# Batch 4's q transposed by DMA from SBUF to SBUF, and a new order of all engines from the first product of h on

## The chip, the cores and the metric

The kernel runs on one core of one Trainium2 chip. The core has a matrix engine (TensorE, PE in the profile; its weight loads are PEld), a vector engine (VectorE, DVE), an engine for activations (ScalarE, ACT), GpSimd (POOL) and SyncE (SP). Here POOL and SP do little but issue DMAs. All DMAs are served by 16 DMA engines. The matrix engine reads from SBUF and writes to PSUM, which has 8 banks of 2 KB per partition; VectorE and ScalarE carry results out of PSUM.

The metric is the device time of one execution in microseconds, as the median of several runs. Beside it stands one profiled execution, from which the durations come.

## The reference

Eight batches, eight heads, 576 positions, head dimension 64; the model width is 8 x 64 = 512 and the inner width 1024.

```python
kv  = einsum('bhsd,bhse->bhde', k, v)           # 64 x 64 for each batch and head
out = einsum('bhsd,bhde->bhse', q, kv)
rms = sqrt(mean(out * out, axis=-1) + 1e-06)
x   = (out / rms * g_norm)                      # then (b, s, 512)
h   = maximum(x @ w_in, 0)                      # (b, 576, 1024)
c   = conv_w[0]*h[s-1] + conv_w[1]*h[s] + conv_w[2]*h[s+1]
y   = (h * sigmoid(c)) @ w_out                  # (b, 576, 512)
```

All inputs and the output are float32; the kernel works in bfloat16 with float32 sums.

## The kernel before, in words

**Layout.** For each batch q, k and v are loaded by GpSimd with a cast to bfloat16 as `[96, heads, 6*64]`: partition p holds positions 6p to 6p+5. k and v are in the form that `kv` wants. q has to be transposed, so that the head dimension lies on partitions. Heads go in pairs: t = 0 to 3 is a pair, u = 0 or 1 is two pairs.

**The stages for one batch b**, each a small function whose name is used in the order:

- `Lq`, `Lk`, `Lv` (line 300): one load of 576 KB each (batch 1 in two halves). `Li` and `Lo` load the weights w_in (four parts) and w_out (two parts).
- `qt`/`qtp` (407): TensorE transposes of one u into PSUM; batches in `QP` use `by_parity` (387), 12 transposes of 96x128. `qc` (416) copies the result to the SBUF tile `qT`, on VectorE or (with `:1`) on ScalarE.
- `dq` (437): in place of `qt` and `qc`, for the batches in `QD`: SyncE issues one DMA transpose of one u from the SBUF tile of q to the SBUF tile `qT`.
- `kv` (352): 48 small matmuls into one bank. `kvn` (444) and `ky` (456) copy the result to SBUF, straight and with the halves exchanged; `kx` does the exchange by DMA instead.
- `oq` (460): the product of q and kv for one pair. `sq` (491) squares it on ScalarE, `oc` (500) copies it to SBUF.
- `ss` (570), `ln` (584), `sl` (590), `sp` (600): the sums of squares, the reciprocal root, its split in two bfloat16 parts, and its spread over partitions by TensorE. `mu` (625) multiplies and writes x. For batches 6 and 7 the factor goes through DRAM (`fw`, `fr`). Batches 0 and 1 use an older path (`ot`, `on`, `nl`, `mu0`).
- `hm` (637): one 128-wide slice f of h for a batch, 8 matmuls. `ha` and `hb` are the same in two parts. `re` (671) is the relu, on ScalarE or (`:1`) VectorE.
- `ta` (697), `aa` (706), `ab` (712): the convolution on VectorE; `sg` (739) the sigmoid on ScalarE; `mg` (751) the product with h. These go in five groups c of one or two batches.
- `om` (759): one output tile of 128 rows, 8 matmuls of 128x512 (for the first and last pair of batches in two halves of 4, `.0` and `.4`); `ea` (768) copies it out of PSUM and `st` (798) stores it from SyncE. The last rows go by `oh`, `eh`, `sh`.
- `unread` (424): matmuls whose result nobody reads (fills).

**What sets the order.** The string `ORDER` (line 68 on) lists every step by name. The loop at line 802 runs through it and issues the instructions; then the program ties each instruction to the one before it on the same engine. So the string is the order of every engine, of SyncE and GpSimd too, whose DMAs go out in that order. A token `name.args:choice@slots` gives the engine choice and the places: banks of PSUM, or slots of a ring of SBUF tiles. A step that takes a slot waits for the last users of that slot. The q tiles of the batches share two slots (`q0`, `q1`), k and v likewise two each, `qT` four, the output rows eight.

Before the change SyncE's list begins with dq.5.0, dq.5.1, a store, dq.7.0. GpSimd's list from batch 2 on is Li.2, Lq.2, Lv.2, Lk.2, Lv.3, Lk.3, Lq.3, Lo.0, Lo.1, Lq.4, Lv.4, Lk.4, Lq.5, Lv.5, Lk.5, Lq.7, Lv.7, Lk.7, Lv.6, Lk.6, Lq.6. Lq.7 takes q's slot 0, which batch 4 held; Lq.6 takes slot 1, which batch 5 held.

Of the kernel before, what the change touches and what calls it, by code (L numbers as in the profile page):

```python
# [52 lines left out]
BF16 = mybir.dt.bfloat16  # L53
# [6 lines left out]
QD = (5, 6, 7)  # L60
QP = (2, 3, 4)
# [11 lines left out]
Lq.1.2 ot.0.3@2 sqh.0.3.0@0 mu0.0.2 qt.1.0@0 sqh.0.3.1 onh.0.3.0@6 qc.1.0@0 onh.0.3.1 nlh.0.3.0@1 nlh.0.3.1 ha.0.2@4
muh.0.3.1 ha.0.3@0 muh.0.3.0 ps dg.6 Lv.1.2 hm.0.6@6 dg.7 hb.0.2 re.0.2:1 hm.0.7@2 hb.0.3 re.0.6 cm.0.6@4 sg.0.6@0
re.0.7:1 kv.1.0.2@6 kvc.1.0.2.0@0 ta.0.2@1 kvc.1.0.2.1 cm.0.7@2 ot.1.0@4 hm.0.0@6 sg.0.7 re.0.3:1 ta.0.3 aa.0.1
re.0.0:1 unread.3.1@0 ta.0.0@2 sq.1.0@0 on.1.0@2 nl.1.0@0 hm.0.1@0 ot.1.1@6 qt.1.1@2 re.0.1 ab.0.1 kv.1.2.2@0 mu0.1.0
sq.1.1@0 kvc.1.2.2.1 on.1.1@4 qc.1.1@0 kvc.1.2.2.0 ot.1.3@2 mg.0.3 Li.2 ta.0.1 ot.1.2@0 nl.1.1@0 mu0.1.1 hm.0.4@4
sq.1.2@0 sq.1.3@1 Lq.2.0@0 re.0.4 pl on.1.2@6 Lv.2.0@0 aa.0.0 on.1.3@4 nl.1.2@0 ab.0.0 mu0.1.2 nl.1.3@1 hm.0.5@6
qtp.2.0@0 mu0.1.3 re.0.5:1 ha.1.2@4 sg.0.1 hb.1.2 qc.2.0@0 ta.0.4@0 hm.1.6@2 sg.0.3 qtp.2.1@0 Lk.2.0@0 ta.0.5 aa.0.2
sg.0.0 hm.1.1@6 ab.0.2 re.1.2 qc.2.1@1 sg.0.2 ha.1.3@4 ta.1.2@3 re.1.1 sg.0.4 sg.0.5 hb.1.3 mg.0.0 re.1.6 hm.1.7@6  # L80
al.h1@1 kv.2.0.4@0 re.1.7 mg.0.1 re.1.3 kvn.2.0.4:1 ky.2.0.4.1 hm.1.0@2 hm.1.5@6 ky.2.0.4.0 re.1.0 ta.1.6@1 re.1.5
oq.2.0@0 oq.2.1@4 sq.2.0@0 sq.2.1@1 hm.1.4@2 mg.0.2 ta.1.7 ta.1.3 ta.1.0@0 oq.2.2@6 Lv.3.0@1 oc.2.0:1@0 aa.1.3 oc.2.1
# [42 lines left out]
def kernel(  # L125
# [725 lines left out]
```

## Time and profile before

| | us |
|---|---|
| median of 3 runs | 176.46 |
| lowest and highest run | 175.97, 176.98 |
| profiled execution: span | 174.7 |
| last matmul ends, start of the last copy | 171.36 |
| busy PE, DVE, ACT in the span | 164.6, 151.8, 144.0 |

The span is that of the profiled execution, first to last recorded instruction or transfer; the run time stands 1.7 us above it. How to read what follows: a group row names the line of the code, the engine, what is written and read, how often, then busy time and mean duration, then the idle time in front of these instructions. The chain of waits is followed back from the last instruction; in order of time each piece has its start, its length and its place. A DMA issue row ends with the microseconds from the issue to the landing. In queue rows q0 is the queue of GpSimd's loads and q1 that of SyncE's transfers; the share is of 16 engines and can pass 100% because packets overlap.

### The profile page before, as it was taken

Reading aid. Unit: us, or ns where it says so; the run is one execution under the profiler, and the core shown is the slowest. Engines: PE = TensorE matmul, PEld = TensorE weight load, DVE = VectorE, ACT = ScalarE, POOL = GpSimd, SP = SyncE. Lnnn points to the kernel's source line nnn. Section 1 sums busy time; section 2 is a strip of 40 time slices with the busy share of each in tenths; the row PEclk is TensorE's granted clock in tenths of the full one; section 3 lists DMA queues with packets and bytes.
Section 4 is the critical chain, followed back from the end, with each engine's and each line's share of the span. In section 5 each row is a group of like instructions: output and inputs, shape, how many; then the busy total and the mean of one; then the engine's idle time right before and its main releaser. Section 6 shows DMA issues by size and latency. Waiting matters only on the chain.

```text
span 174.7 us, 3978 instructions
## 1 busy us (share of the span) xinstructions
PE 164.6 (94%) x1590; PEld 100.1 (57%) x1607; DVE 151.8 (87%) x248; ACT 144.0 (82%) x224; POOL 30.8 (18%) x54
## 2 busy tenths in 40 slices
PE   6988997899799999999999999999999999999992
PEld 2545765685644687744677774545687654444451
DVE  4166799999999999999999999999989999998520
ACT  4578897999999999999999998999988629766132
POOL 7994705313130001810000000000000000000000
PEclk9999999999999999999999999999999999999999
DMA  5999999999999999999999390477694400076285
GB/s 151 182 186 198 200 202 203 205 204 204 208 203 205 203 204 164 162 196 191 190 203 234 72 261 6 149 188 181 173 268 161 152 0 4 23 277 235 90 322 196
DMA packets 37450, 30.81 MB, mean 176 GB/s; under 512 B 8608, under 2 KB 32952, under 8 KB 37432
## 3 DMA queue, kind: packets, MB, share of 16 engines
q0 software_dynamic: 21760, 15.96, 60.7%
q1 hardware_dynamic: 15632, 14.59, 29.6%
q8 instruction: 12, 0.20, 0.4%
q14 instruction: 6, 0.05, 0.1%
q10 hardware_dynamic: 40, 0.01, 0.0%
HBM read 34.88 MB, written 9.73 MB: 255 GB/s over the span
## 4 chain that ended last, share of the span: by engine, by line
PE 76%; DVE 9%; DMA 4%; POOL 4%; ACT 2%; issue 2%; POOLq 0%; ACTq 0%
PE bank L764 35%; PE bank L643 30%; DMA w_in_sb<-in_moe_w_in_dram 4%; PE bank L361 3%; PE bank L467 2%; DVE taps L703 1%; DVE qT L346 1%; POOL q_sb L245 1%; DVE taps L709 1%; DVE h L754 1%; PE bank L606 1%; DVE taps L702 1%; POOL v_sb L245 1%; POOL k_sb L245 1%; PE bank L781 1%
## 5 line engine op out<-in xcount | busy, mean ns | idle before, releaser
L643 PE MATMUL bank<-xT,w_in_sb 128*128 128x288 bf16 x480 | 63.6, 286 | 0.3 <-ACT root L545 0.2
L764 PE MATMUL bank<-w_out_sb,h 128*128 128x512 bf16 x267 | 62.4, 379 | 0.8 <-issue 0.3
L643 PEld LDWEIGHTS <-w_in_sb 128*128 128x128 bf16 x480 | 46.0, 98 | 14.9 <-issue 1.6
L748 ACT ACTIVATE taps<-taps,cwn 128x1152 bf16<-128x1152 bf16 (+1 forms) x38 | 39.7, 1078 | 7.4 <-DVE taps L715 7.3
L764 PEld LDWEIGHTS <-h 128*128 128x128 bf16 x280 | 26.4, 98 | 31.0 <-issue 1.2
L649 ACT ACTIVATE h<-bank 128x576 bf16<-128x576 f32 x48 | 30.2, 656 | 3.0 <-PE bank L643 2.8
L344 ACT ACTIVATE row<-bank 128x512 f32<-128x512 f32 (+1 forms) x29 | 16.3, 595 | 8.8 <-PE bank L764 6.0
L754 DVE TENSOR_TENSOR h<-h,taps 128x2304 bf16<-128x2304 bf16 (+1 forms) x20 | 22.0, 1109 | 0.6 <-ACT taps L748 0.6
L709 DVE TENSOR_TENSOR taps<-taps 128x2304 bf16<-128x2304 bf16 (+1 forms) x19 | 21.5, 1134 | 0.2
L715 DVE TENSOR_TENSOR taps<-taps,h 128x2304 bf16<-128x2304 bf16 (+1 forms) x19 | 21.5, 1131 | 0.2
L496 ACT ACTIVATE sq<-bank 128x576 bf16<-128x576 f32 x28 | 17.8, 663 | 0.6 <-PE bank L467 0.3
L703 DVE TENSOR_SCALAR taps<-h,cwn 128x1152 bf16<-128x1152 bf16 (+1 forms) x38 | 17.8, 467 | 0.0
L702 DVE TENSOR_SCALAR taps<-h,cwn 128x1152 bf16<-128x1152 bf16 (+1 forms) x38 | 17.4, 457 | 0.3 <-ACT h L649 0.2
L217 ACT ACT_TABLE_LOAD x12 | 15.4, 1283 | 2.6 <-issue 2.4
L651 DVE TENSOR_SCALAR h<-bank 128x576 bf16<-128x576 f32 x16 | 11.8, 752 | 1.7 <-PE bank L643 0.8
L344 ACT ACTIVATE o<-bank 128x576 f32<-128x576 f32 x19 | 12.8, 674 | 0.0
L632 DVE SCALAR_TENSOR_TENSOR xT<-o,cw,bank 128x576 bf16<-128x576 f32 x16 | 12.2, 808 | 0.1
L304 POOL DMA_DIRECT2D q_sb<-in_q_dram x8 | 6.2, 770 | 30.2 <-PE bank L391 29.4
L430 PE MATMUL bank<-fill 128*128 128x512 bf16 x25 | 9.0, 481 | 1.5 <-DVE fill L232 1.5
L346 DVE COPY row<-bank 128x512 f32<-128x512 f32 (+1 forms) x8 | 5.4, 672 | 4.4 <-PE bank L781 2.4
L361 PE MATMUL bank<-v_sb,k_sb 96*64 96x64 bf16 x384 | 8.3, 197 | 0.7 <-ACT sq L496 0.5
L361 PEld LDWEIGHTS <-k_sb 96*64 96x64 bf16 x384 | 7.1, 112 | 2.9 <-issue 2.2
(94 smaller groups left out, 148.8 us busy)
## 6 DMA issues: line engine op xcount, KB each, us to landing
out_dram<-row SPq DMA_DIRECT2D x35, 256.0 KB, 2.6
q_sb<-in_q_dram POOLq DMA_DIRECT2D x6, 576.0 KB, 15.2
v_sb<-in_v_dram POOLq DMA_DIRECT2D x6, 576.0 KB, 14.6
k_sb<-in_k_dram POOLq DMA_DIRECT2D x6, 576.0 KB, 16.6
factor<-factor SPq DMA_DIRECT2D x8, 288.0 KB, 5.4
w_in_sb<-in_moe_w_in_dram POOLq DMA_DIRECT2D x4, 256.0 KB, 9.0
w_out_sb<-in_moe_w_out_dram POOLq DMA_DIRECT2D x2, 512.0 KB, 18.3
q_sb<-in_q_dram POOLq DMA_DIRECT2D x4, 144.0 KB, 4.7
```

What stands on the lines that cost most here:

```text
L344: nc.scalar.activation(to, fr, AX.Copy)
L361: nc.tensor.matmul(ps[i][i * D:(i + 1) * D, t - t0, :], k_sb[:, 2 * t + i, r * D:(r + 1) * D], v_sb[:, 2 * t + i, r * D:(r + 1) * D], star ...
L496: nc.scalar.activation(in_order(b, s), product(b, t), AX.Square)
L643: nc.tensor.matmul(ps[:, e, :HS], w_in_sb[:, t, f * P:(f + 1) * P], x[:, t, e * HS:(e + 1) * HS], start=(t == 0), stop=(t == NT - 1))
L649: nc.scalar.activation(to, fr, AX.Relu)
L702: nc.vector.tensor_scalar_mul(tap[:, 0, f % 2, :n, 8:8 + S], h[:, f], cwn[:, 0, f:f + 1])
L703: nc.vector.tensor_scalar_mul(tap[:, 1, f % 2, :n, :S], h[:, f], cwn[:, 2, f:f + 1])
L709: nc.vector.tensor_add(tap[:, 1, :, :n, :S], tap[:, 0, :, :n, 7:7 + S], tap[:, 1, :, :n, 1:1 + S])
L715: nc.vector.tensor_add(y, y, h[:, 2 * j:2 * j + 2])
L748: nc.scalar.activation(y, y, AX.Sigmoid, scale=cwn[:, 1, f:f + 1])
L754: nc.vector.tensor_mul(h, h, T["tap", c, j][:, 1, :, :n, :S])
L764: nc.tensor.matmul(T["om", p, m], h[:, f, m * P:(m + 1) * P], w_out_sb[:, f, :], start=(f == 0), stop=(f == NF - 1))
```

## The change

Batch 4 moves from the batches whose q TensorE transposes (`QP`) to those whose q is transposed by DMA (`QD`): qtp.4.0, qtp.4.1, qc.4.0 and qc.4.1 go, dq.4.0 and dq.4.1 come. The tiles for kvn and kvx are made ahead of the order for all batches, which issues no instruction. From the first product of h on, the order string is a new one for all engines.

```diff
-QD = (5, 6, 7)
-QP = (2, 3, 4)
+QD = (4, 5, 6, 7)
+QP = (2, 3)
 QUAD = QD + QP
...
+    for b in QUAD:
+        T["kvn", b] = consts.tile([P, NT, D], BF16, name=f"kvn{b}")
+        T["kvx", b] = consts.tile([P, NT, D], BF16, name=f"kvx{b}")
+
     @op
     def kvn(b, t0, n):
-        if t0 == 0:
-            T["kvn", b] = consts.tile([P, NT, D], BF16, name=f"kvn{b}")
-            T["kvx", b] = consts.tile([P, NT, D], BF16, name=f"kvx{b}")
```

The order string is replaced as a whole from ha.0 on. The new lists of the queues, and TensorE's from batch 4's kv to batch 7's:

```
SyncE:  dq.4.0 dq.4.1 dq.5.1 dq.5.0 dq.7.1 st.0.1 dq.7.0 dq.6.0 dq.6.1 st.0.3 st.0.6 st.0.8 st.0.0 kx.7.0.4.0 st.0.7 kx.7.0.4.1 ...
GpSimd: Li.2 Lv.2@0 Lq.2@0 Lk.2@0 Lv.3@1 Lk.3@1 Lq.3@1 Lo.0 Lo.1 Lq.4@0 Lv.4@0 Lk.4@0 Lq.5@1 Lk.5@1 Lv.5@0
        Lq.7@0 Lq.6@1 Lv.7@1 Lk.7@1 Lk.6@0 Lv.6@0
TensorE: kv.4 sp.3.0 hm.2.7 hm.3.5 oq.4.1 oq.4.0 hm.3.4 hm.2.6 hm.3.6 hm.3.3 hm.3.1 oq.4.3 oq.4.2
        kv.5 hm.3.2 om.0.8.0 hm.2.3 oq.5.2 oq.5.0 om.0.6.0 hm.3.7 om.0.8.4 om.0.4.0 oq.5.3 oq.5.1 om.0.6.4
        om.0.5.0 ss.4 ss.5 hm.2.1 om.0.4.4 hm.2.0 om.0.5.4 sp.4.1 kv.7 om.0.7.0 sp.4.0 om.0.7.4 ...
```

dq.4.0 takes qT's slot 0 and dq.4.1 slot 2, after batch 3's products; dq.5.1 takes slot 1, dq.5.0 slot 3. The engine choices differ too: of 64 relus VectorE does 14 (before 16), of 35 row copies 4 (before 7), of 12 copies for batch 0 and 1's kv 7 (before 4), of 8 exchanged copies 4 (before 3). The fill before the last matmuls stands behind them now. At the end of the string:

```diff
-om.3.1.4 eh.3.8.0:1@4 st.2.5 ea.3.2@1 st.3.5 st.3.2 ea.3.3@2 st.3.3 om.3.7.4 ea.3.1@0 unread.1.2@0 sh.3.8.0 ea.3.7@0
-st.3.1 st.3.7 oh.3.8.1 eh.3.8.1 sh.3.8.1
+ea.3.1@3 st.3.1 st.3.6 om.3.7.4 ea.3.7@2 st.3.7 om.3.2.4 ea.3.2@1 st.3.2 oh.3.8.0@2 eh.3.8.0@5 sh.3.8.0 oh.3.8.1
+eh.3.8.1 unread.1.2@7 sh.3.8.1
```

More of the change, by code (lines that the diff above doesn't have):

```diff
@@ L73 @@
[L73 to L82, printed above, removed]
@@ new lines @@
+re.1.2 aa.0.2 ab.0.2 hm.1.5@2 sg.0.1 mg.0.0 hm.1.7@4 re.1.7 Lo.0 qtp.2.1@6 qc.2.1:1@2 hm.1.6@0 re.1.6:1 ta.1.6@2
+ta.1.7 sg.0.4 re.1.5 Lo.1 qtp.2.0@4 qc.2.0@0 kv.2.0.4@6 ky.2.0.4.1 kvn.2.0.4 ky.2.0.4.0 ta.1.2@0 hm.1.1@0 ha.1.3@2
+aa.1.3 sg.0.5 re.1.1 oq.2.2@6 sq.2.2@0 oc.2.2@0 hb.1.3 re.1.3:1 ta.1.3 aa.1.1 hm.1.4@4 re.1.4 ta.1.4@1 ta.1.5 ab.1.3
+oq.2.0@2 sq.2.0@3 oc.2.0@2 ab.1.1 Lq.4.0@0 hm.1.0@6 re.1.0 oq.2.3@4 sq.2.3@2 oc.2.3 unread.3.1@0 kv.3.0.4@2
+ky.3.0.4.1:1 ky.3.0.4.0:1 kvn.3.0.4 aa.1.2 oq.2.1@6 sq.2.1@4 oc.2.1 qtp.3.1@4 qc.3.1@0 qtp.3.0@2 qc.3.0@2 ss.2@6
```

87 lines of the change are left out of this document (46 added, 41 removed).

## The prediction

> **What bounds the kernel now.** First the page: busy times, the slices, the shares of the chain.
>
> ```profile
> PE 164.6 (94%) x1590; PEld 100.1 (57%) x1607; DVE 151.8 (87%) x248; ACT 144.0 (82%) x224; POOL 30.8 (18%) x54
> ...
> GB/s 151 182 186 198 200 202 203 205 204 204 208 203 205 203 204 164 162 196 191 190 203 234 72 261 6 149 188 181 173 268 161 152 0 4 23 277 235 90 322 196
> ...
> PE 76%; DVE 9%; DMA 4%; POOL 4%; ACT 2%; issue 2%; POOLq 0%; ACTq 0%
> ```
>
> TensorE holds the chain for 76% of the span, but DMA stands at 200 to 208 GB/s in slices 5 to 15 (one slice is 4.37 us: 17 to 66 us) without a dip: a saturated resource beside PE. Next the stages, from the busy times by stretch:
>
> ```profile
> 16.50:48.10 31.60, 28.32 (x409) 20.90 (x411) 29.54 (x60) 29.54 (x53) 11.46 (x23) 1.00 1.32 204
> 48.10:80.00 31.90, 31.59 (x340) 18.98 (x343) 31.33 (x53) 31.46 (x54) 6.29 (x8) 1.00 1.27 191
> 171.40:174.70 3.30, 0.00 (x0) 0.92 0.48 173
> ```
>
> Columns: length; PE, PEld, DVE, ACT, POOL busy; granted clock; DMA share; GB/s (the last row is of PE alone). PE idles 31.60 - 28.32 = 3.28 us in the first stage and 0.3 us in the second. So a new order can win at most some 3.3 us there; after 48.1 us only less PE work helps. Then the chain of waits in order of time:
>
> ```profile
> 47.29 0.75 DVE qT L346
> ...
> 59.72 0.88 PE bank L361 x48
> ...
> 68.28 0.51 PE bank L391 x12
> ...
> 80.20 0.60 PE bank L578 x16
> ...
> 85.80 0.88 PE bank L361 x48
> 86.68 0.23 PE bank L606 x4
> ...
> 98.51 0.37 PE bank L467 x8
> ...
> 124.15 13.81 PE bank L643 x112
> ...
> 147.52 10.74 PE bank L764 x49
> ...
> 170.66 0.22 PE bank L430
> ...
> 171.36 0.28 ACT row L344
> ```
>
> Until 48 us the chain is DVE, then PE to the end at 171.36. The L361 rows are kv of batch 4 (59.72) and batch 7 (85.80). Unit prices: a product of h (8 matmuls) 13.81/112 x 8 = 0.99 us; half an output tile (4) 10.74/49 x 4 = 0.88; kv 0.88; one fill 0.22.
>
> Behind the kv's stand the loads. GpSimd's timeline, the DMA issues with their us to landing, SyncE's timeline:
>
> ```profile
> 36.03 0.79 POOL L304 DMA_DIRECT2D q_sb<-in_q_dram  x1 [4.11 <-PE bank L391]
> ...
> 40.69 0.77 POOL L304 DMA_DIRECT2D k_sb<-in_k_dram  x1
> 47.18 0.77 POOL L304 DMA_DIRECT2D q_sb<-in_q_dram  x1 [5.72 <-PE bank L391]
> ...
> 48.80 0.78 POOL L304 DMA_DIRECT2D k_sb<-in_k_dram  x1
> 69.11 0.77 POOL L304 DMA_DIRECT2D q_sb<-in_q_dram  x1 [19.53 <-PE bank L391]
> ...
> 70.63 0.77 POOL L304 DMA_DIRECT2D k_sb<-in_k_dram  x1
> ```
>
> ```profile
> q_sb<-in_q_dram POOLq DMA_DIRECT2D x1, 576.0 KB, 17.3
> ...
> k_sb<-in_k_dram POOLq DMA_DIRECT2D x1, 576.0 KB, 18.4
> ...
> q_sb<-in_q_dram POOLq DMA_DIRECT2D x1, 576.0 KB, 14.7
> ...
> k_sb<-in_k_dram POOLq DMA_DIRECT2D x1, 576.0 KB, 20.2
> ...
> q_sb<-in_q_dram POOLq DMA_DIRECT2D x1, 576.0 KB, 8.0
> ...
> k_sb<-in_k_dram POOLq DMA_DIRECT2D x1, 576.0 KB, 13.5
> ...
> qT<-q_sb SPq DMA_TRANSPOSE x1, 7.9
> ...
> qT<-q_sb SPq DMA_TRANSPOSE x1, 11.6
> ```
>
> ```profile
> 61.94 6.91 SPq L439 DMA_TRANSPOSE qT<-q_sb  x2
> ...
> 77.15 2.20 SPq L439 DMA_TRANSPOSE qT<-q_sb  x1
> ```
>
> Issue plus landing, row by row: q4 53.3, k4 59.1, q5 61.9, k5 69.0, q7 77.1, k7 84.1 us. k4 lands 0.6 us before kv of batch 4, k7 1.7 us before kv of batch 7. The transposes of q5 go out when q5 is there (61.94; first of two: 7.9 us), that of q7 at 77.15; this one has v7, k7 and more loads behind it and takes 11.6.
>
> How loads and transposes share, by queue, in 50 to 60 (loads alone), 84 to 86 (both), 100 to 102 us (transposes alone):
>
> ```profile
> q0 software_dynamic: 2678, 2.02, 130.8%
> ...
> q0 software_dynamic: 377, 0.28, 90.2%
> q1 hardware_dynamic: 378, 0.10, 36.6%
> ...
> q1 hardware_dynamic: 1464, 0.37, 103.8%
> ```
>
> Columns: packets, MB, share. A load of 576 KB (0.59 MB) at 0.202 MB/us is 2.9 us. Beside a transpose loads get 0.14 MB/us, the transpose 0.05: its 0.29 MB then last 5.9 us and cost the loads (0.202 - 0.14) x 5.9 = 0.37 MB, that is **1.8 us each**. Alone a transpose needs 0.29/0.185 = 1.6 us.
>
> **The change part by part.** The sum is against the profiled execution: last matmul 171.36, span 174.72; the median, 176.46, is 1.74 above that span, and I carry the difference over.
>
> *Transposes off TensorE.*
>
> ```profile
> L391 PE MATMUL bank<-ident,q_sb 96*128 96x96 bf16 x72 | 3.9, 206 | 0.1
> ...
> L344 ACT ACTIVATE qT<-bank 128x1152 bf16<-128x1152 bf16 x1 | 1.1, 1130 | 0.0
> ```
>
> Twelve take 0.51 us (68.28), two such groups go: PE -1.02, of the 72 remain 48. ScalarE loses one copy (1.1), VectorE the other; the new order also moves three ea and two re from VectorE to ScalarE, three kvc and a ky back. Both run beside PE; I count nothing. The fill before the last matmuls (170.66) moves behind them: -0.22. PE work in all: -1.24. The kvn tiles made earlier issue nothing.
>
> *The front.* Batch 1's norms and relus are rearranged; batch 2's loads go out earlier. Bounds: nothing to -3.28, the idle. Earlier issue brings nothing, since that queue is full up to k5. I take 0.6: that is by how much kv of batch 4 can come forward before k4's landing at 59.1 ends it, whatever the front wins.
>
> *Two more DMA transposes, and where they stand.* SyncE now has dq.4.0, dq.4.1, dq.5.1, dq.5.0, dq.7.1, one store, dq.7.0, dq.6.0, dq.6.1. dq.4.0 waits for q4 and goes out at 53.3. Before, no transpose was in flight until 61.9. Now v4, k4, q5, k5, v5 stand beside the batch 4 pair, and the batch 5 pair follows when q5 lands.
>
> *Three new waits on GpSimd.* (1) Lv.5 now takes v's slot 0 and waits for kv of batch 4; it goes out near 61 and joins the queue behind k5, so it costs nothing yet. (2) Lq.7 waits for both transposes of q4, no longer for TensorE. (3) **Lq.6 is put ahead of Lv.7, Lk.7, Lk.6 and Lv.6**, and q's slot 1 is free only when dq.5.1 and dq.5.0 have landed. Behind it waits Lk.7, for that kv of batch 7, and behind kv all of PE, in order.
>
> The sum, step by step:
> 1. v5: five loads after 53.3 are 14.5 us, the batch 4 pair 3.6: 71.4. Kv of batch 5 starts at 71.5 (before: 71.0).
> 2. dq.5.0 lands, X: 53.3 + 14.5 + 4 x 1.8 = 75.0. Low end, four at 1.6: 74.2. High end: dq.4.0 11.6 us as the loaded row (64.9), dq.4.1 another 5.9 (70.8), then 4.2 us beside q7 (0.21 MB) and the remaining 0.37 MB alone (2.0): 77.0. I take 75.0; the loads run out near 71, as they did under the 7.9 us row.
> 3. k7: before, from Lq.7's issue at 69.11 to k7's landing at 84.1 were 15.0 us: three loads from an empty queue with one transpose among them. Now the same three follow Lq.6's issue: X + 15.0 = 90.0. Ends: 13.2 without that transpose, 16.8 with another (dq.7.1 and dq.7.0 both fall here).
> 4. PE, without that wait: kv of batch 5 at 71.5, then kv 0.88, five products 4.93, eight half tiles 7.0, four oq (two pairs at 0.37), two sums 0.60, a spread 0.23: 14.4, so kv of batch 7 at 85.9. It waits 4.1 us, to 90.0.
> 5. Rest: before, 171.36 - 85.80 = 85.56. Now one half tile more stands behind kv of batch 7 (om.0.7.0, +0.88) and the fill is gone (-0.22): 86.2. Last matmul 176.2, +4.8.
>
> **176.46 + 4.8 = 181.3 us.** Ends: 74.2 + 13.2 gives 178.7, 77.0 + 16.8 gives 185.1. VectorE and ScalarE gain slack during the wait. dq.4.0 (61 to 65) is wanted by oq near 64, dq.4.1 by 70: a wait of up to 1 us there lies ahead of v5's and is not added. At the end the two last stores go out together; 0 to +0.3, I take 0.
>
> [...]
>
> **The rivals.**
> *Cheap transposes.* Each costs the loads what 0.29 MB of load costs, 1.45 us. X = 53.3 + 14.5 + 5.8 = 73.6, the leg 14.65, k7 88.2, last matmul 174.4: **179.5**. For: alone, 0.185 MB/us is near the loads' 0.202. Against: the row of 84 to 86 us. [...]
>
> *The load of q6 is no wall.* If X + leg stays under 85.9 (dq.5.0 by 71), only v5 counts: 71.5 + 14.4 + 86.2 = 172.1, **177.2**. Against: X would need transposes that cost half.
>
> *Faster: DMA has room.* The transposes slip between the loads at under 0.9 us for all four, v5 is there by 68.7 and dq.5.0 by 68. Then PE sets the end: -1.24 - 0.6, **174.6**. For: PE holds 76% of the chain. Against: the 200 to 208 GB/s. It decides at kv of batch 7: once k7 lands more than 1.8 us behind PE's arrival there, the gain is spent.
>
> *The clock falls in the wait.* The granted clock was 0.92 in the 3.3 us after the last matmul: if it halves, it did so 2.8 us in. A wait of 4.1 us reaches that. With as long a recovery, 2.8 us at half rate, 1.4 are lost: **182.7**. Against: 1.00 in both stage rows; but PE idled there in 3.3 us of short pieces only. [...]
>
> **How the numbers follow.** Forecast 0.46, cheap transposes 0.13, clock 0.12, no wall 0.12, faster 0.17. Faster by over 0.5% is the one case: 0.17. No wall (+0.4%) is mostly within 0.5%, about what a measurement here can tell from no change: 0.10 same, its rest slower: 0.73. The range leaves out the faster case and the top tail: from 176.0, below no wall, to 185.1.
>
> **What would show it.** In the profile after: k_sb's load of batch 7 lands near 90 and TensorE's longest wait, some 4 us, stands before an L361 group, released by DMA k_sb; GpSimd's wait before Lq.6 is for a transpose, near 75 us; L391 has x48; the batch 4 transposes land 8 to 12 us and later after issue. Wrong if the L361 groups start without waits, or if a second wait (a store behind dq.6.1 that keeps an output row's slot) is longer than these.

## The result and the profile after

The change makes the kernel **slower by 10.7%**: 198.6 us median of 4 runs (195.5 to 201.9) against 176.5, ratio 1.107 (95% interval 1.102 to 1.112). In two of these four runs, in some runs of five kernels below with the new front (the profiled ones of e5_front and e17_newfront_early among them) and in one of the kernel before, the mean granted clock was lower (here 0.947, against 0.956 and 0.974) and the time some per cent longer; ratios leave such runs out, and where too few are left the lowest runs are given. The prediction was 181.3 us with a range up to 185.1: the direction was right, the size was not.

The profiled execution of the changed kernel took 195.54 us with a span of 193.7. First its page: busy times, the granted clock by slice, the shares of the chain.

```profile
PE 169.2 (87%) x1566; PEld 100.5 (52%) x1583; DVE 150.6 (78%) x244; ACT 146.9 (76%) x226; POOL 30.2 (16%) x54
...
PEclk9999999999999999999669699999999999999999
...
PE 36%; DMA 28%; DVE 16%; issue 8%; ACT 5%; POOL 4%; SPq 2%; ACTq 0%; POOLq 0%; DVEq 0%
```

TensorE fell from 76% of the chain to 36%, and DMA rose from 4% to 28%. The clock, at nine tenths or more in every slice before, dips in three slices from 92 to 111 us (4.84 us each). TensorE's timeline, with start, length and, in brackets, the wait ahead and its releaser, says where the time went:

```profile
63.34 0.95 PE L361 MATMUL bank<-v_sb,k_sb 96*64 96x64 bf16 x48
...
75.70 0.95 PE L361 MATMUL bank<-v_sb,k_sb 96*64 96x64 bf16 x48 [1.21 <-DMA v_sb<-in_v_dram]
...
93.54 0.39 PE L607 MATMUL bank<-wparts,spread 32*128 32x288 bf16 x1 [3.32 <-ACT row L344]
94.63 0.43 PE L607 MATMUL bank<-wparts,spread 32*128 32x288 bf16 x3 [0.69 <-ACT h L650]
94.98 1.49 PE L361 MATMUL bank<-v_sb,k_sb 96*64 96x64 bf16 x48
...
107.14 0.43 PE L607 MATMUL bank<-wparts,spread 32*128 32x288 bf16 x4 [3.73 <-ACT h L650]
107.68 4.50 PE L644 MATMUL bank<-xT,w_in_sb 128*128 128x288 bf16 x24
...
112.34 0.95 PE L361 MATMUL bank<-v_sb,k_sb 96*64 96x64 bf16 x48
...
188.55 1.91 PE L782 MATMUL bank<-w_out_sb,h 128*128 128x384 bf16 x16
```

The same view of the kernel before, for its four kv groups:

```profile
59.65 0.95 PE L361 MATMUL bank<-v_sb,k_sb 96*64 96x64 bf16 x48
...
70.94 0.95 PE L361 MATMUL bank<-v_sb,k_sb 96*64 96x64 bf16 x48
...
85.73 0.95 PE L361 MATMUL bank<-v_sb,k_sb 96*64 96x64 bf16 x48
...
94.27 0.95 PE L361 MATMUL bank<-v_sb,k_sb 96*64 96x64 bf16 x48
```

So kv of batch 4 starts 3.7 us later than before (63.34 - 59.65), kv of batch 5 4.8 later, kv of batch 7 9.3 later (94.98 - 85.73) and kv of batch 6 18.1 later; the last matmul whose result is used ends at 190.5 and not at 171.4, 19.1 later. Two stretches make 13.3 us of it: 4.5 between batches 5 and 7 and 8.8 between batches 7 and 6. Neither wait there is for a load. The first, 3.32 us, is for a ScalarE row copy (`ea`), the second, 3.73, for a relu behind another row copy. ScalarE's timeline shows what those copies wait for:

```profile
92.89 0.60 ACT L344 ACTIVATE row<-bank 128x512 f32<-128x512 f32 x1 [4.39 <-DMA out_dram<-row]
...
105.95 0.60 ACT L344 ACTIVATE row<-bank 128x512 f32<-128x512 f32 x1 [6.90 <-DMA out_dram<-row]
```

Each copy wants an output row's slot that a store still reads: ea.0.4 waits for st.0.1, ea.0.7 for st.0.8. Why the stores are late is in SyncE's timeline:

```profile
53.32 8.46 SPq L439 DMA_TRANSPOSE qT<-q_sb  x2
64.53 4.53 SPq L439 DMA_TRANSPOSE qT<-q_sb  x2
79.25 3.38 SPq L439 DMA_TRANSPOSE qT<-q_sb  x1
82.73 0.54 SPq L801 DMA_DIRECT2D out_dram<-row  x1
83.39 6.18 SPq L439 DMA_TRANSPOSE qT<-q_sb  x1
89.74 5.82 SPq L439 DMA_TRANSPOSE qT<-q_sb  x1
95.65 4.89 SPq L439 DMA_TRANSPOSE qT<-q_sb  x1
100.59 3.39 SPq L801 DMA_DIRECT2D out_dram<-row  x4
104.08 0.61 SPq L453 DMA_DIRECT2D kvx<-kvn  x1
```

st.0.1 stands behind dq.7.1, which waits for q of batch 7 and goes out at 79.25; the store follows at 82.73. st.0.8 and the crossed kv (kvx) stand behind three more transposes, and these hold SyncE for 6.18 + 5.82 + 4.89 = 16.9 us while the loads of batches 7 and 6 run beside them. How long the transfers then take to land, first for the one store of 82.73, then for the transposes issued from 79 to 101, then for k of batch 7:

```profile
out_dram<-row SPq DMA_DIRECT2D x1, 256.0 KB, 10.1
...
qT<-q_sb SPq DMA_TRANSPOSE x4, 10.9
...
k_sb<-in_k_dram POOLq DMA_DIRECT2D x1, 576.0 KB, 14.1
```

The kernel before, issues from 90 to 104 us, where its last three transposes go out after the loads, two of these stores ahead of them and three behind:

```profile
out_dram<-row SPq DMA_DIRECT2D x5, 256.0 KB, 3.0
...
qT<-q_sb SPq DMA_TRANSPOSE x3, 3.8
```

A store that takes 3 us took 10.1 in the queue behind a transpose and beside the loads: 82.73 + 10.1 = 92.8, just when ScalarE starts again. The place in the queue alone does not do it: the three stores of the kernel before that go out from 101.03 us, right behind two transposes but after the loads, landed in 2.9 us.

The stages after, in the form of the prediction's second fence:

```profile
42.00:52.00 10.00, 6.70 (x122) 4.46 (x122) 9.87 (x22) 8.07 (x15) 1.53 (x2) 1.00 1.28 205
...
90.00:108.00 18.00, 9.93 (x95) 5.58 (x95) 6.75 (x8) 8.17 (x12) 0.00 (x0) 0.79 1.15 213
```

From 90 to 108 TensorE worked 9.93 of 18 us, at a mean granted clock of 0.79. The waits shown above (3.32, 0.69, 3.73) fill the idle 8 but for 0.3 us; the clock is a second loss on top of them.

### The profile page after: what moved, and what is told of

Its sections match the earlier page's. It is cut to its first block, busy times and chain, and to the rows that moved or that the text cites. A ratio compares the mean times of both kernels' runs of the same rounds, so it can differ in the third digit from the quotient of the medians.

```text
span 193.7 us, 3939 instructions
## 1 busy us (share of the span) xinstructions
PE 169.2 (87%) x1566; PEld 100.5 (52%) x1583; DVE 150.6 (78%) x244; ACT 146.9 (76%) x226; POOL 30.2 (16%) x54
## 4 chain that ended last, share of the span: by engine, by line
PE 36%; DMA 28%; DVE 16%; issue 8%; ACT 5%; POOL 4%; SPq 2%; ACTq 0%; POOLq 0%; DVEq 0%
PE bank L765 18%; DMA v_sb<-in_v_dram 14%; PE bank L644 12%; DMA out_dram<-row 7%; DMA w_in_sb<-in_moe_w_in_dram 4%; DMA factor<-factor 3%; DVE taps L703 3%; DVE xT L629 2%; DVE taps L704 2%; DVE taps L716 2%; DVE taps L710 2%; PE bank L361 2%; SPq L801 1%; DVE h L755 1%; POOL q_sb L245 1%
## 5 line engine op out<-in xcount | busy, mean ns | idle before, releaser
L644 PE MATMUL bank<-xT,w_in_sb 128*128 128x288 bf16 x480 | 65.6, 290 | 1.5 <-DVE xT L629 0.6
L765 PE MATMUL bank<-w_out_sb,h 128*128 128x512 bf16 x268 | 64.0, 386 | 1.7 <-ACT rs L588 0.9
L644 PEld LDWEIGHTS <-w_in_sb 128*128 128x128 bf16 x480 | 46.8, 99 | 18.2 <-issue 3.6
L650 ACT ACTIVATE h<-bank 128x576 bf16<-128x576 f32 x50 | 31.5, 656 | 5.0 <-PE bank L644 4.8
L344 ACT ACTIVATE row<-bank 128x512 f32<-128x512 f32 (+2 forms) x33 | 18.5, 586 | 22.0 <-DMA out_dram<-row 11.5
L703 DVE TENSOR_SCALAR taps<-h,cwn 128x1152 bf16<-128x1152 bf16 (+1 forms) x38 | 18.1, 475 | 0.2
L652 DVE TENSOR_SCALAR h<-bank 128x576 bf16<-128x576 f32 x14 | 10.5, 753 | 1.0 <-PE bank L644 0.5
L361 PE MATMUL bank<-v_sb,k_sb 96*64 96x64 bf16 x384 | 8.9, 203 | 2.0 <-DMA v_sb<-in_v_dram 1.4
L361 PEld LDWEIGHTS <-k_sb 96*64 96x64 bf16 x384 | 7.7, 118 | 4.4 <-issue 4.2
L304 POOL DMA_DIRECT2D q_sb<-in_q_dram x8 | 6.0, 750 | 25.7 <-PE bank L391 15.2
L607 PE MATMUL bank<-wparts,spread 32*128 32x288 bf16 x32 | 3.2, 336 | 7.7 <-ACT h L650 4.4
L430 PE MATMUL bank<-fill 128*128 128x512 bf16 x24 | 8.3, 460 | 1.7 <-DVE fill L232 1.5
```

What stands on the lines that cost most here:

```text
L344: nc.scalar.activation(to, fr, AX.Copy)
L361: nc.tensor.matmul(ps[i][i * D:(i + 1) * D, t - t0, :], k_sb[:, 2 * t + i, r * D:(r + 1) * D], v_sb[:, 2 * t + i, r * D:(r + 1) * D], star ...
L644: nc.tensor.matmul(ps[:, e, :HS], w_in_sb[:, t, f * P:(f + 1) * P], x[:, t, e * HS:(e + 1) * HS], start=(t == 0), stop=(t == NT - 1))
L650: nc.scalar.activation(to, fr, AX.Relu)
L703: nc.vector.tensor_scalar_mul(tap[:, 0, f % 2, :n, 8:8 + S], h[:, f], cwn[:, 0, f:f + 1])
L765: nc.tensor.matmul(T["om", p, m], h[:, f, m * P:(m + 1) * P], w_out_sb[:, f, :], start=(f == 0), stop=(f == NF - 1))
```

## Experiments

Each kernel ran beside the kernel before on the same chip. All orders below are edits of the order string. The table gathers where TensorE starts the four kv groups in the profiled execution, and the time.

| kernel | kv 4 | kv 5 | kv 7 | kv 6 | us, median | ratio to before (95%) |
|---|---|---|---|---|---|---|
| before | 59.7 | 70.9 | 85.7 | 94.3 | 176.5 | |
| after | 63.3 | 75.7 | 95.0 | 112.3 | 198.6 | 1.107 (1.102 to 1.112) |
| e1_rows | 65.0 | 76.1 | 93.6 | 104.7 | 193.2 | 1.096 (1.085 to 1.107) |
| e2_loads | 64.7 | 76.0 | 94.3 | 112.3 | 195.3 | 1.108 (1.095 to 1.121) |
| e3_both | 67.1 | 78.2 | 92.9 | 102.4 | 191.1 | 1.084 (1.073 to 1.095) |
| e4_before_dq4 | 59.8 | 72.8 | 89.3 | 97.8 | 180.2 | 1.022 (1.011 to 1.034) |
| e5_front | 69.5 | 80.7 | 95.5 | 104.1 | 184.3 (182.4, 186.1) | |
| e6_rest | 60.2 | 75.0 | 95.1 | 114.3 | 198.8 | 1.123 (1.088 to 1.159) |
| e7_q4pe | 64.8 | 77.2 | 92.9 | 111.7 | 197.7 (195.2, 200.3) | |
| e8_kvx | 64.8 | 75.9 | 90.6 | 101.5 | 190.4 (188.1, 192.6) | |
| e9_syncorder | 63.8 | 75.4 | 92.9 | 104.0 | 186.7 | 1.055 (1.038 to 1.072) |
| e10_sync_loads | 63.5 | 75.5 | 90.2 | 101.0 | 186.4 | 1.053 (1.037 to 1.070) |
| e11_rest_repaired | 60.9 | 75.5 | 91.8 | 101.6 | 185.8 | 1.050 (1.044 to 1.056) |
| e12_before_sync | 59.2 | 70.5 | 89.5 | 100.9 | 182.8 | 1.033 (1.027 to 1.039) |
| e13_v5 | 59.8 | 73.1 | 89.4 | 102.9 | 187.1 | 1.046 (1.027 to 1.066) |
| e14_v5_q4pe | 62.3 | 74.6 | 89.3 | 98.8 | 182.7 | 1.022 (1.004 to 1.040) |
| e15_newfront_q4pe | 65.7 | 78.0 | 92.7 | 102.2 | 189.3 (186.6, 192.1) | |
| e16_q4pe_early | 60.6 | 73.0 | 87.7 | 98.8 | 182.6 | 1.031 (1.025 to 1.037) |
| e17_newfront_early | 66.6 | 80.6 | 95.2 | 104.7 | 188.8 (185.2 to 193.6) | |

### The waits one at a time: rows, loads, both

The theory from the trace: the two stores are the wall. The rival: the load of q of batch 6 ahead of v and k of batch 7, as predicted.

e1_rows gives the two row copies slots of their own, so that no copy waits for those stores:

```diff
-ea.0.4@6
+ea.0.4@8
-ea.0.7@4
+ea.0.7@9
```

> The changed kernel with two more slots for output rows, so that the copies of output tiles 4 and 7 (ea.0.4, ea.0.7) no longer wait for the stores of tiles 1 and 8; every DMA keeps its place. Theory S (stores behind transposes on SyncE hold output rows, ScalarE waits for them 4.4 and 6.9 us, and the clock falls meanwhile): both waits go, PE reaches batch 7's kv near 91 and then waits for k7, which lands near 92.5; after it nothing stops, the clock stays up: 184 to 186. Rival L (the wall of loads that the prediction named): k7 and v6 still set the times, so only a part of the first wait goes: 191 to 194.

Measured 193.2 us, in the range of rival L: the row waits are gone, but little is won. TensorE's waits in e1_rows show their successors (total, times, longest):

```profile
PE bank L361 <- DMA k_sb<-in_k_dram: 2.7, 1, 2.7
PE bank L468 <- DMA kvx<-kvn: 2.5, 1, 2.5
```

The first is for k of batch 7, as rival L has it. The second, at 108.3 us right behind kv of batch 6, is for the crossed kv of batch 7, whose second half goes out on SyncE at 106.07, behind the same transposes and stores. The row slots were only one of the things that the late queue held up.

e2_loads moves one load on GpSimd:

```diff
-Lq.7 Lq.6 Lv.7 Lk.7 Lk.6 Lv.6
+Lq.7 Lv.7 Lk.7 Lq.6 Lk.6 Lv.6
```

> The changed kernel with GpSimd's loads in the order Lq.7, Lv.7, Lk.7, Lq.6, Lk.6, Lv.6 (Lq.6 no longer ahead of batch 7's v and k); SyncE's order kept. Theory S: k7 lands some 6 us earlier, but kv of batch 7 stands behind the wait for the first store, so it gains nothing; q6 lands about 6 us later, with it the two transposes of q6 and the stores behind them, so the wait for tile 8's store grows: 197 to 202. Rival L: kv of batch 7 comes about 4 us earlier and so does the end: 190 to 192.

Measured 195.3 us, no change that these runs could show, and outside both ranges: ScalarE's waits for rows remain and kv of batch 6 starts at 112.3 as before. The load that the prediction made the wall is worth nothing while SyncE is late.

e3_both has both edits.

> Both edits: two more row slots and batch 7's k and v ahead of Lq.6. Theory S with the load wall as a second, smaller wait: kv of batch 7 at 90 to 91 (TensorE's own pace from batch 5's kv at 75.7), and no wait for a store: 181 to 183. Rival L: as e2, 186 to 190, if the stores had only waited where PE waited anyway.

Measured 191.1 us, above both ranges: kv of batch 7 comes at 92.9 without a wait, and the crossed kv takes over:

```profile
PE bank L468 <- DMA kvx<-kvn: 3.3, 1, 3.3
```

e8_kvx adds to e3_both copies from the bank in place of the four kvx transfers:

```diff
-kvn.7.0.4 kx.7.0.4.0 ... kx.7.0.4.1
+kvn.7.0.4 ky.7.0.4.0:1 ky.7.0.4.1
-kvn.6.0.4:1 kx.6.0.4.0 kx.6.0.4.1
+kvn.6.0.4:1 ky.6.0.4.0:1 ky.6.0.4.1
```

> The kernel with both repairs (two more output rows, q of batch 6 behind k of batch 7), and the crossed kv of batches 7 and 6 copied from the bank by ScalarE and VectorE, as in batches 2 to 5, in place of four transfers that stood behind transposes and stores on SyncE. With both repairs alone 191.1 us, with 3.3 us of TensorE's wait put down to these transfers. Theory K (that wait is on the path): 187 to 188.5 us. Rival (the wait gives way to the next one, the transposes that the products of q of batches 7 and 6 want): 190 to 191.5 us.

Measured 188.1 and 192.6 us. The lower run lies in the range of theory K: the wait was on the path, some 2.5 us against the lower run of e3_both (190.7, on another chip).

### SyncE's order alone, and its converse

e9_syncorder moves only SyncE's instructions:

```diff
-dq.4.0 dq.4.1 dq.5.1 dq.5.0 dq.7.1 st.0.1 dq.7.0 dq.6.0 dq.6.1 st.0.3 st.0.6 st.0.8 st.0.0 kx.7.0.4.0 st.0.7 kx.7.0.4.1 kx.6.0.4.0 kx.6.0.4.1
+dq.4.0 dq.4.1 dq.5.1 dq.5.0 st.0.1 dq.7.0 st.0.3 st.0.6 st.0.8 st.0.0 kx.7.0.4.0 st.0.7 kx.7.0.4.1 dq.7.1 kx.6.0.4.0 kx.6.0.4.1 dq.6.0 dq.6.1
```

> The kernel after the change with SyncE's queue alone in another order: the first store goes ahead of the batch 7 transposes, and the second transpose of batch 7 and both of batch 6 go behind the five stores and behind the crossed kv of batch 7 and batch 6, as they stand in the kernel before. Every other engine keeps the order after the change, q of batch 6 is still loaded ahead of v and k of batch 7. Theory S (from 79 us on SyncE's row sets the end: a store and the kvx transfers wait behind transposes that each hold SyncE 5 to 6 us): ScalarE's waits for output rows and TensorE's for kvx go, kv of batch 7 stays at 92 to 93 us, where k of batch 7 lands, kv of batch 6 comes to 101 to 103, and the time to 184 to 187 us. Rival N (another wait stands as late, as after each single repair so far): 190 us or more.

Measured 186.7 us (185.5 and 187.9), in the range of theory S. SyncE's timeline, TensorE's, and a stage of e9_syncorder:

```profile
69.17 0.53 SPq L801 DMA_DIRECT2D out_dram<-row  x1
79.44 2.35 SPq L439 DMA_TRANSPOSE qT<-q_sb  x1
```

```profile
92.90 0.95 PE L361 MATMUL bank<-v_sb,k_sb 96*64 96x64 bf16 x48 [2.78 <-DMA k_sb<-in_k_dram]
```

```profile
90.00:108.00 18.00, 15.22 (x200) 9.62 (x197) 12.92 (x18) 13.13 (x18) 0.00 (x0) 0.91 0.78 160
```

The first store goes out at 69 and not at 83, no wait for a row is left, and kv of batch 6 comes at 104.0 in place of 112.3. TensorE works 15.2 of the 18 us that held 9.9. What remains is the prediction's own wait, 2.78 us for k of batch 7.

e10_sync_loads adds the edit of e2_loads.

> The same order of SyncE, and q of batch 6 loaded behind k of batch 7. If theory S holds and the load of q of batch 6 is the next wall: kv of batch 7 at 89 to 90, 181 to 184 us. If TensorE itself is by then as late as the load (its front is 4 to 5 us behind): no gain over the kernel with SyncE's order alone, 185 to 187 us.

Measured 186.4 us (185.3 and 187.6). In the trace kv of batch 7 starts at 90.2 without a wait, 2.7 us earlier, and the span of the profiled execution is 2.7 us shorter (183.5 against 186.2), but the medians differ by 0.3 only; each kernel had two runs, 2.3 or 2.4 us apart, so a gain up to some 2 us is neither shown nor excluded.

e12_before_sync is the converse, the kernel before with the two queues in the new manner:

```diff
-SyncE:  dq.5.0 dq.5.1 st.0.0 dq.7.0 kx.7.0.4.1 kx.7.0.4.0 st.0.5 st.0.1 dq.7.1 kx.6.0.4.0 kx.6.0.4.1 dq.6.0 dq.6.1
+SyncE:  dq.5.0 dq.5.1 dq.7.0 st.0.0 dq.7.1 dq.6.0 dq.6.1 kx.7.0.4.1 kx.7.0.4.0 st.0.5 st.0.1 kx.6.0.4.0 kx.6.0.4.1
-GpSimd: Lq.7 Lv.7 Lk.7 Lv.6 Lk.6 Lq.6
+GpSimd: Lq.7 Lq.6 Lv.7 Lk.7 Lv.6 Lk.6
```

> The converse: the kernel before the change, batch 4 on TensorE, with only the queues of SyncE and GpSimd in the new manner: q of batch 6 loaded right behind q of batch 7 and ahead of v and k of batch 7, all four transposes of batches 7 and 6 ahead of the crossed kv of batches 7 and 6 and of four of the stores. Theory S: this alone makes the old kernel slower by 6 to 14 us, 182 to 190 us, with TensorE waiting for kvx or for rows behind the transposes. Rival (the order of queues needs the late front or batch 4's transposes to do harm): below 179 us.

Measured 182.8 us, 3.3% over the kernel before (2.7 to 3.9): in the range of theory S. Its ScalarE, TensorE and SyncE timelines repeat the pattern in a kernel with the old front and batch 4 on TensorE:

```profile
88.86 0.60 ACT L344 ACTIVATE row<-bank 128x512 f32<-128x512 f32 x1 [5.01 <-DMA out_dram<-row]
```

```profile
89.51 1.49 PE L361 MATMUL bank<-v_sb,k_sb 96*64 96x64 bf16 x48 [4.16 <-ACT row L344]
```

```profile
78.43 0.59 SPq L800 DMA_DIRECT2D out_dram<-row  x1
79.13 6.76 SPq L439 DMA_TRANSPOSE qT<-q_sb  x1
86.07 5.34 SPq L439 DMA_TRANSPOSE qT<-q_sb  x1
91.50 4.96 SPq L439 DMA_TRANSPOSE qT<-q_sb  x1
```

The store is again about 10 us behind its issue (78.43 to 88.86), and kv of batch 7, which takes 0.95 us elsewhere, takes 1.49 behind the wait of 4.16. The three transposes hold SyncE 17.1 us, as in the changed kernel. The load of q of batch 6 was moved in the same step, but it could account for 1.4 us of this wait at most: TensorE stood from 85.4 to 89.5, and k of batch 7 had landed at 86.8 (73.2 + 13.6). So the order of the two queues does harm in the old kernel too, 5.8 us here, and SyncE's part alone 9 to 10 in the changed kernel (195.5 against 185.5 by the lowest runs).

### Batch 4's transposes by DMA

e4_before_dq4 is the kernel before with batch 4 alone by DMA:

```diff
-QD = (5, 6, 7)
-QP = (2, 3, 4)
+QD = (4, 5, 6, 7)
+QP = (2, 3)
-qtp.4.0@6 qc.4.0:1@0 ... dq.5.0@2 ... dq.5.1@1 ... qtp.4.1@4 qc.4.1@0
+dq.4.0@0 dq.4.1@3 ... dq.5.0@2 ... dq.5.1@1
```

> The kernel before, with nothing but batch 4's q by DMA: dq.4.0 and dq.4.1 first in SyncE's list, qtp.4 and qc.4 gone, the rest of the order as before. If the DMA transposes themselves cost little (theory S: it is the order around them): PE loses 1.0 us of work, batch 5's k lands 2 to 4 us later (71 to 73) and batch 5's kv waits 0 to 2 us: 175.5 to 178. If the transposes beside the loads are the cause: 181 to 186, with oq of batch 4 and kv of batch 5 and 7 all waiting for DMA.

Measured 180.2 us, 2.2% over before (1.1 to 3.4), between the two ranges. TensorE's timeline shows a product of q waiting for dq.4.1:

```profile
72.42 0.28 PE L467 MATMUL bank<-qT,kvn 64*64 64x288 bf16 x1 [1.93 <-DMA qT<-q_sb]
```

Behind this wait the granted clock was 0.57 for four microseconds, which by 4 x 0.43 takes another 1.7 us, an estimate (same form as the stages above):

```profile
74.00:78.00 4.00, 4.00 (x21) 2.63 (x20) 1.57 (x4) 3.68 (x6) 3.55 (x5) 0.57 1.06 169
```

e7_q4pe does the opposite in the changed kernel, batch 4 back on TensorE, all else as after:

```diff
-dq.4.0@0 ... dq.4.1@2 ... re.2.5:1 kv.4.0.4@4 ... re.2.7
+re.2.5:1 qtp.4.0@0 qc.4.0@0 kv.4.0.4@4 ... re.2.7 qtp.4.1@0 qc.4.1@2
```

> The order after the change, with batch 4's q transposed on TensorE again (12 + 12 products and two copies, +1.0 us of TensorE), so that six transposes by DMA remain and the first goes out when q of batch 5 is there. Theory T (the two transposes of batch 4 delay v of batch 5, the transposes behind them and so the first store): v of batch 5 lands by 71, the first store goes out before 76, 182 to 187 us. Theory O (the order alone: stores and kvx behind transposes, q of batch 6 ahead of the other loads): 190 to 195 us, with the same waits of ScalarE for output rows.

Measured 195.2 and 200.3 us: the lower run lies at the end of theory O's range. SyncE's timeline of e7_q4pe:

```profile
77.33 2.00 SPq L439 DMA_TRANSPOSE qT<-q_sb  x1
79.39 0.62 SPq L801 DMA_DIRECT2D out_dram<-row  x1
```

With two transposes fewer the first store still goes out at 79.4, since dq.7.1 ahead of it waits for q of batch 7. While that wall stands, the step that gives the change its name has no part in the 19 us that these runs could show (195.2 against 195.5 by the lowest runs).

### Front and rest apart

e5_front takes the new order up to kv of batch 4 (its dq's taken out, batch 4's transposes put in as in e7_q4pe), then the old one; four tap slots and two row slots are renamed where the orders meet. The seam against the order after:

```diff
 hm.2.5@0 re.2.5:1
-kv.4.0.4@4 sg.1.1 sp.3.0@2,6 mu.3.0.0 ...
+qtp.4.0@0 qc.4.0:1@0 al.x2@0 sg.1.1 sg.1.0 kv.4.0.4@5 ...
```

> The order after the change up to kv of batch 4, then the rest in the order before the change; batch 4's q by TensorE as before the change, no transpose by DMA before those of batch 5. Tap, row and bank slots are renamed where the two orders meet, nothing else differs. In the profile after the change kv of batch 4 started 3.6 us later than before it. Theory R (the new front is only late because the transposes of batch 4 and the loads move beside it): 175 to 177.5 us, kv of batch 4 near 60. Theory F (the front's order itself costs the 3.6 us, VectorE being full there): 178.5 to 181 us, kv of batch 4 at 62.5 to 64.

e6_rest takes the old order up to the place of qtp.4.0, then the new one, with dq.4.0 and dq.4.1; two tap slots and a row slot are renamed. The seam against the order before:

```diff
 mu.2.1.1 sl.1@0
-qtp.4.0@6 qc.4.0:1@0 hm.2.4@0 om.0.2.4 ...
+aa.1.2 dq.4.0@0 dq.4.1@2 Lq.5.0@1 dq.5.1@1 sg.1.2 om.0.2.4 ...
```

> The counterpart: the order before the change up to the place where batch 4's q was transposed, then the rest in the order after the change, with both transposes of batch 4 by DMA. If the losses add, front 3.6 and rest 15: 190 to 192 us, kv of batch 4 near 60, and TensorE still waits for output rows before kv of batch 7 and of batch 6. If what sets the end after 80 us is SyncE's row of transposes and stores, whatever the front does: 193 to 196 us. If the rest is only bad behind the late front: below 187 us.

e5_front: 182.4 and 186.1 us, above both ranges, with kv of batch 4 at 69.5 in the slower run, the profiled one. e6_rest: 198.8 us, above all three ranges; the old front gains nothing, kv of batch 7 is at 95.1 as after. That fits the second case best: what sets the end behind 80 us is SyncE's row, whatever the front does. So the parts do not add while that wall stands.

e11_rest_repaired is e6_rest with the edits of e9_syncorder and e2_loads.

> The front before the change, the rest after it with both transposes of batch 4 by DMA, SyncE's order repaired and q of batch 6 behind k of batch 7. Without SyncE's repair this front and rest took 198.8 us. If the front's loss then shows as such: 178 to 181 us, the price of the batch 4 transposes beside the loads (180.2 us in the order before). If v of batch 5, which waits on kv of batch 4 for its slot, sets the pace: 182 to 186 us, as with the new front.

Measured 185.8 us: the old front starts kv of batch 4 at 60.9 and is no better at kv of batch 5 (75.5). TensorE waited 2.49 us there for v of batch 5. e13_v5 undoes the slots of v:

```diff
-Lk.5.0@1 ... Lv.5.0@0 ... Lv.7.0@1 ... Lv.6.0@0
+Lv.5.0@1 Lk.5.0@1 ... Lv.7.0@0 ... Lv.6.0@1
```

> The front before the change, the repaired rest (185.8 us), and v's slots as before the change: v of batch 5 takes slot 1, so it goes out ahead of k of batch 5 and not behind kv of batch 4. If v of batch 5 was the wall at 75 us (TensorE worked 7.3 of the 11.7 us from 63.3 to 75): kv of batch 5 at 72 to 73 us, 181 to 183 us, near the 180.2 us of the old order with batch 4 transposed by DMA. If the batch 4 transposes hold TensorE up there on their own (oq of batch 4 waiting for them): 184.5 to 186 us.

Measured 187.1 us, ratio 1.046 against 1.050, above both ranges. Kv of batch 5 does come 2.5 us earlier (73.1), but kv of batch 6 comes no earlier (102.9), and at batch 5 the next wait takes over, in TensorE's timeline of e13_v5:

```profile
72.70 0.31 PE L468 MATMUL bank<-qT,kvn 64*64 64x288 bf16 x1 [2.13 <-DMA qT<-q_sb]
```

That is the same product waiting for dq.4.1 as in e4_before_dq4. Ahead of batch 6 another wait for an output row comes back (ScalarE 2.30 us for a store, TensorE 1.89 behind it). e14_v5_q4pe puts batch 4 back on TensorE there (the edit of e7_q4pe):

> The same with batch 4's q on TensorE again. All that is left of the change is the order of TensorE, ScalarE and VectorE after the front, and the fill moved to the end. If the batch 4 transposes cost 3 to 4 us, as in the old order: 177 to 179.5 us. If the rest's order of the compute engines costs more by itself: over 180.5 us.

Measured 182.7 us, above the first range; in the same batch of runs 4.3 us less than e13_v5. So with the old front the two transposes cost about 4 us, waits and clock together, as in the old order. e15_newfront_q4pe is e14 with the new front:

> The front after the change with the same repaired rest, v's slots as before and batch 4's q on TensorE: it differs from the run before only in the front. If the new front costs its 3.6 us by itself: 181 to 183.5 us, kv of batch 4 at 63 to 64. If the lateness of kv of batch 4 is made good behind it: as the run before, within 1 us.

Measured 186.6 and 192.1 us, above both cases. In the two profiles every kv starts 3.4 us later than in e14_v5_q4pe (65.7, 78.0, 92.7, 102.2 against 62.3, 74.6, 89.3, 98.8), and the lower run is 4.1 us longer. In both, TensorE waits for the bank of the first transposes put in (1.69 and 1.22 us, <-DVE h L652), which is an artefact of the place. e16_q4pe_early and e17_newfront_early put qtp.4.0 where the bank is free (the second line is e16's, the last e17's); qtp.4.1 stays:

```diff
-re.2.5:1 qtp.4.0@0 qc.4.0@0 kv.4.0.4@4
+sl.1@0 qtp.4.0@6 qc.4.0:1@0
...
+om.0.0.4 qtp.4.0@4 qc.4.0:1@0
```

> The front before the change and the repaired rest with v's slots as before and batch 4's q on TensorE, its first transposes now placed where the kernel before has them, ahead of the bank wait that stood before kv of batch 4 in the last run. What is left of the change is the order of TensorE, ScalarE and VectorE in the rest and the fill at the end. Theory M (the order of the compute engines is nearly neutral, the 4 us of the last run were mostly that wait): within 1.5 us of the kernel before, kv of batch 4 at 60. Rival C (this order costs by itself): 2.5 us or more over the kernel before.

> The same with the front after the change: the front is the only difference. If the front costs its 3.6 us by itself: 3 to 4.5 us over the run with the old front, at every kv. If TensorE makes it good: under 1.5 us.

e16: 182.6 us, 5.5 over the 177.1 of the kernel before: rival C. The front, v's slots and batch 4's way of transposing are those of before, SyncE's order is the repaired one of e9, and from 48 us on no wait of TensorE for a transfer is left in its timeline. So what remains costs 3.1% (2.5 to 3.7): the order of the compute engines in the rest above all, with the place of qtp.4.1 and the smaller differences of the queues in it. TensorE's timeline of e16_q4pe_early:

```profile
65.49 0.31 PE L468 MATMUL bank<-qT,kvn 64*64 64x288 bf16 x1 [1.33 <-ACT kvn L344]
67.62 5.06 PE L644 MATMUL bank<-xT,w_in_sb 128*128 128x288 bf16 x40 [0.92 <-DVE qT L346]
...
95.02 0.30 PE L607 MATMUL bank<-wparts,spread 32*128 32x288 bf16 x4 [1.30 <-ACT h L650]
...
135.85 8.14 PE L644 MATMUL bank<-xT,w_in_sb 128*128 128x288 bf16 x63 [0.69 <-DVE xT L629]
```

Small waits for copies: kvn of batch 4, which the new order puts behind both exchanged copies, a relu, a norm whose factor is late; 0.92 and a smaller one of 0.35 are for the q copies put back, so they belong to the repair and not to the new order. With four of 0.18 to 0.35 they make 5.3 us, where the kernel before waits 0.3 after 48.1 us. e17: 185.2 to 193.6 us; the lowest run is 2.8 us above e16's (182.3), just short of the 3 to 4.5 expected; no interval can be given.

## Why the prediction was wrong, step by step

**The failed step** is the sum's fifth: 86.2 us from kv of batch 7 to the last matmul, and with it the fourth, that TensorE reaches that kv at 85.9 and waits there for a load. Measured: kv of batch 7 at 94.98 with no wait for k, and 95.5 us behind it. The prediction listed SyncE's new order and named the store in it, but gave it no price, and counted each moved transpose only as a load on the DMA engines, not as an instruction that holds SyncE (6.18, 5.82 and 4.89 us in the trace) in front of stores and kvx. It even wrote down the sign, "a store behind dq.6.1 that keeps an output row's slot", as a thing that would make it wrong, and made no rival of it. What the runs showed in its place: e9_syncorder against the changed kernel, where SyncE's order alone costs 9 to 10 us, and e12_before_sync against the kernel before, where the order of both queues costs 5.8 us, with TensorE's wait for an output row 4.16 us long.

**TensorE's work**: L391 has x48, as predicted. Its -1.24 us do not show, because TensorE isn't the bound any more.

**The front**: taken as 0.6 gained, bounded by nothing lost. It lost 3.7. From 42 to 52 us TensorE works 6.70 us (8.50 in the same stretch before) while VectorE is full in both (9.87 and 9.89) and ScalarE, which waits 1.66 us there for a copy of VectorE, falls from 9.92 to 8.07. The lower bound was the mistake: a new order can use a full VectorE worse. By itself the front costs about 3 to 4 us (2.8 in e17, 4.1 in e15, by the lowest runs; e5_front, with its seam, about 7); beside batch 4's DMA transposes it costs nothing, since kv of batch 5 then starts at 75.5 with either front (e10, e11).

**Step 1**, v of batch 5 at 71.4: it landed at 75.6. "It goes out near 61" hung on kv of batch 4, and with the late front this became 65.3. The row names a transpose that landed about then; but in e6_rest and e7_q4pe, with kv of batch 4 at 60.18 and 64.84, the load goes out at 62.14 and 66.81, 2.0 us behind it as here, so kv releases it:

```profile
65.31 0.78 POOL L304 DMA_DIRECT2D v_sb<-in_v_dram  x1 [14.11 <-DMA qT<-q_sb]
...
76.94 0.77 POOL L304 DMA_DIRECT2D q_sb<-in_q_dram  x1 [6.40 <-DMA qT<-q_sb]
```

**Step 2**, X = 75.0: dq.5.0 went out at 66.8, landed 9.6 us later at 76.4, and Lq.6 followed at 76.94; within the ends. **Step 3**, k of batch 7 15.0 us after that issue, at 90.0: it landed 15.6 after it, at 92.5 (78.4 + 14.1). Mechanism and size were right, and it bound nothing: e2_loads, which takes the wall away, changes nothing. Only behind the repaired queue does the wait appear, 2.78 us (e9).

**"VectorE and ScalarE gain slack"**: they hold TensorE up instead. With everything else near the kernel before, the new order of the compute engines is the main part of 5.5 us (e16). No rival had it.

**The clock** came as its rival said, though behind other waits: 0.79 from 90 to 108 us, after waits of 3.32 and 3.73. Between kv of batches 7 and 6 lie 17.4 us, before 8.5; 4.0 of the 8.8 more are waits (3.73, 0.22) and 0.9 is the half tile moved there, so about 4 are left for the clock, an estimate. Single rows show it: kv of batch 7 took 1.49 us in place of 0.95, and three products of h at 107.68 took 4.50 where the prediction's 0.99 each make 3.0. Finer stretches of the trace show the halving itself:

```profile
90.30:93.40 3.10, 0.00 (x0) 0.00 (x0) 0.52 (x1) 0.51 (x2) 0.00 (x0) 1.00 1.24 232
93.50:100.20 6.70, 5.75 (x63) 2.68 (x64) 3.05 (x5) 5.52 (x7) 0.00 (x0) 0.50 1.28 194
100.40:107.00 6.60, 3.00 (x25) 2.24 (x23) 2.36 (x2) 1.05 (x3) 0.00 (x0) 1.00 1.04 225
107.20:110.40 3.20, 3.09 (x16) 1.90 (x16) 2.72 (x5) 2.71 (x4) 0.00 (x0) 0.50 0.26 92
110.60:112.30 1.70, 1.70 (x17) 1.12 (x15) 0.34 (x1) 0.74 (x2) 0.00 (x0) 1.00 0.00 0
```

The clock fell 3.3 and 3.7 us after the last matmul ahead (ends 90.2 and 103.4), in the kernel before 2.8 us after it (0.50 from 174.2 us). A recovery of 2.8 us, as in that rival's sum, was the prediction's assumption and no run shows it: the two stretches at 0.50 are 6.8 and 3.4 us long. Shorter waits were followed by a lower clock too: 0.57 from 74 to 78 us behind waits of 1.93 (e4) and 2.13 us (e13), and 0.58 from 94 to 98 us behind 2.78 (e9).

**The account.** Against the kernel before: the rest of the order, the compute engines' above all, 3.1% (e16); front and batch 4's transposes, which hide each other, about 2% more (e10, e11 and e13 at 1.046 to 1.053); SyncE's order and the load of q of batch 6 the other 5 to 6% up to 1.107. What stays open: in e16 some 2 us are lost after kv of batch 6, and wait rows show 1.0 of them; the gain of the load order alone; and why a transpose holds SyncE as long as it does. No kernel here beats the one before.

## What to carry to other kernels

Read the list of an issuing engine as a queue with a price for each entry: whatever stands behind a transfer that waits for a load, or that is slow to issue beside loads, is as late as that transfer (dq.7.1 went out at 79.25 us, st.0.1 behind it at 82.73), and a store can hold up TensorE through an output row's slot (3.32 us here, 4.16 in e12). A wall that is removed is worth only the distance to the next one, so repair the queue and not the single wait (e1, e2 and e3 against e9). When a whole order is replaced, price it stage by stage with a lower bound below zero: a saturated engine has no slack to gain (VectorE was busy 9.87 of the 10 us in which TensorE fell from 8.50 to 6.70).

## What was not expected of the hardware

- **A DMA transpose holds the engine that issues it.** SyncE was held 4.9 to 6.8 us by each transpose that followed another one beside a full stream of loads (after, 83.4 to 100.5 us; e12), 1.8 to 3.4 us by the first after a pause beside such loads (after, 53.32 and 79.25), and 1.3 to 1.8 us where the loads had ended (before, 92.8 to 101.0 us). The landing of those issued from 79 to 101 us took 10.9 us against 3.8.
- **A store behind a transpose in the same queue and beside loads** took 10.1 us to land (after; 10.4 in e12), against 2.9 behind transposes without loads.
- **Waits of TensorE of about 2 us were followed by a lower clock.** A single one of 1.93 us was (e4, 0.57), one of 1.69 us in e14 was not (1.00 from 52 to 75 us). In e17 TensorE's waits from 42 to 52 us are 0.67, 1.14, 0.41 and 0.28 long, and the clock was 0.88 there (0.88 in e15 too). With the old front all eight profiled executions have a granted clock of 1.00 from 30 to 63.3 us; with the new front nine of eleven fall below it in some stage there. TensorE's waits from 42 to 52 us are 0.67, 1.13, 0.41 and 0.89 long in the changed kernel, none over 1.13 us; there the clock stayed at 1.00, as in e7, the second of the two. One stage of e17_newfront_early:

```profile
52.00:63.30 11.30, 11.03 (x67) 4.59 (x68) 7.70 (x15) 9.18 (x16) 0.22 (x1) 0.80 1.32 203
```

That short waits, close together, cause it is argued from this count and was not tried by itself.
